# One issue order read from a table, in place of rules: memory-augmented attention plus a SiLU feed-forward layer

## The chip, the cores and the metric

One core of a Trainium2 chip. The time is that of one launch on the device in microseconds (us); lower is better. TensorE does the matmuls, ScalarE (ACT) the activations, VectorE (DVE) and GpSimd (POOL) the element-wise work, SyncE (SP) and ScalarE issue the transfers (DMA).

## The reference, cut to what matters

```python
def reference(A_x, A_wq, A_wk, A_wv, A_wo, A_beta, B_x, B_w1, B_w2):
    xn = _layernorm(A_x)              # 2048 tokens x 512
    return A_x + attention(xn, A_wq, A_wk, A_wv, A_wo, A_beta) + ffn(xn, B_w1, B_w2)

# attention: 32 heads of 16; four segments of 512 tokens. Causal softmax within
# a segment, and a memory M, z carried on from segment to segment:
#   num = phi(q) @ M ; den = phi(q) . z ; o = g*num/den + (1-g)*softmax(...)@v
#   M += phi(k)^T v  ; z += sum phi(k)            phi(t) = t+1 if t>0 else exp(t)
# ffn: silu(xn @ w1) @ w2, 1792 wide
```

The first segment's four token tiles of 128 (x0 to x3) must be loaded, normalised and transposed, and half of w_q loaded, before the first query, key and score matmuls can run.

## The kernel before

The kernel does not emit instructions directly. It builds some 1,700 **tasks** (engine, estimated duration, what they depend on, buffers taken and freed, and a function that emits the instructions). A simulation then picks at each moment a task for each engine, and the functions are called in the simulated order. So the simulation decides only one thing on the chip: the order of the instructions in each engine's stream.

```python
class Sched:
    ENGS = ("SP", "ACTQ", "PE", "ACT", "DVE", "POOL")     # ACTQ: transfers issued by ScalarE
    ...
    def run(self):
        free = {e: 0.0 for e in self.ENGS}                # each has its own time line
        ...
        def pick(e):                                      # rules: scores first, then PV, then by due
            ...
        while left:
            for e in self.ENGS:
                while free[e] <= now + 1e-9:
                    t = pick(e)
                    ...
                    order.append((now, t))

    def load_x(t, n, eng, due, vis, after=()):
        def fn():
            e = nc.sync if eng == "SP" else nc.scalar     # "ACTQ" is ScalarE's own stream
            e.dma_start(...)
    load_x(0, 1, "SP", 0, 3.4)        # last number: when it is taken to have landed
    load_x(1, 1, "ACTQ", 0, 3.55)
    load_x(2, 1, "SP", 0, 3.6)
    load_x(3, 1, "ACTQ", 0, 3.8)
    ...
    ld_q = [load_w(*halves(w_q, A_wq, C2, 0), "ACTQ", 0, 6.4)]
    ...
    # in ln(): the statistics of token tile 2 on ScalarE
    m = A("ACT", 0.6, f_m, [xl[t]], due, label="mean")    # waits for x2
    m = A("ACT", 0.69, f_q, [m], due, label="sq")
    ...
    def first_tile(w, loads, due, label, hf):             # first key or query tile, in halves hf
        b = Buf(banks)
        for j in (2 * hf, 2 * hf + 1):                    # one piece for each token tile
            c, o = slice(j * P, (j + 1) * P), slice((j % 2) * P, (j % 2) * P + P)
            def f(c=c, o=o):
                for ki in range(DT):
                    mm(b.tile[:, o], w[:, ki, 0:P], xnT_b[0].tile[:, ki, c], ki == 0, ki == DT - 1)
            pcs.append(A("PE", 0.3, f, [xnT_done[0][j], loads], ...))
    ...
    for t, k in sc.run():
        k.fn()
```

The softmax here doesn't subtract the row's maximum and nothing guards it: scores larger than these inputs give would overflow.

Of the kernel before, what the change touches and what calls it, by code (L numbers as in the profile page):

```python
# [14 lines left out]
P = 128  # L15
# [25 lines left out]
STARVE = 0.55  # L41
# [4 lines left out]
LOWB = 1  # L46
# [8 lines left out]
LAST = 1  # L55
PVW = 0.0
# [9 lines left out]
SW = 0.1  # L66
SEM = 0.05
SHIFT = {
    "POOL": {
        ("", 4): -31.1, ("kB", 16): 80.6, ("pq", 0): -10.1, ("pq", 2): 18.3, ("pq", 6): 8.4,  # L70
        ("pq", 10): 6.2, ("M52", 1): -7, ("Mbf", 2): 35.4,
    },
    "PE": {
        ("tr", 1): 9.5, ("k1", 0): -13.1, ("k2", 0): 22.9, ("q2", 0): -12.4, ("q3", 0): -0.3,
        ("h0.0", 0): -54.5, ("h0.2", 0): 30.1, ("h0.3", 0): -7.3, ("h0.6", 0): 11.6,
        ("h0.7", 0): 10.6, ("h0.12", 0): -10.2, ("k4", 0): -0.9, ("q6", 0): 9.6, ("k7", 0): -11.8,
        ("v10", 0): -5.8, ("v11", 0): -6.8, ("M0", 0): 5, ("w2.1", 0): 1.8, ("w2.3", 0): -1.8,
        ("wo.3", 0): 20.3, ("h1.1", 0): 7.4, ("h1.3", 0): -16.4, ("h1.4", 0): 3.5,
        ("h1.5", 0): 1.8, ("h1.6", 0): 10.2, ("h1.7", 0): -10.6, ("h1.8", 0): -3.7,
        ("k8", 0): -7.8, ("v22", 0): -12.9, ("M1", 0): -7, ("psN", 0): -5.6, ("w2.4", 0): -30.2,  # L80
        ("w2.7", 0): -3.9, ("wo.4", 0): 28.9, ("wo.5", 0): 3.2, ("wo.6", 0): -27.6,
        ("wo.7", 0): -42.5, ("PV8", 0): 5.8, ("PV9", 0): 8.6, ("PV10", 0): 7.3, ("h2.0", 0): -7.2,
        ("h2.1", 0): 10.7, ("h2.5", 0): -7.9, ("h2.6", 0): -13.3, ("h2.9", 0): 7.9,
        ("q12", 0): -2.8, ("q13", 0): 4.8, ("k14", 0): 1.6, ("k15", 0): 15, ("v32", 0): 26.1,
        ("M2", 0): 29, ("w2.10", 0): 4, ("wo.9", 0): -27.9, ("wo.10", 0): 17.9, ("PV12", 0): 31.2,
        ("PV13", 0): 47.7, ("h3.0", 0): -14.7, ("h3.1", 0): 46.3, ("h3.2", 0): 38.7,
        ("h3.4", 0): -37.3, ("h3.7", 0): 26.5, ("h3.10", 0): -7.1, ("h3.12", 0): 16.4,
        ("h3.13", 0): 40.6, ("outT2", 0): -24.2,
    },
    "DVE": {  # L90
        ("stats", 3): 4.5, ("stats", 10): -3.1, ("xn", 5): -0.9, ("k0", 0): 11.1,
        ("EO", 26): 36.4, ("glu", 45): -20.7, ("tailA", 1): 4.6,
    },
    "SP": {
        ("Z", 15): -16.3, ("Z", 26): 8.7, ("den", 12): -6.9, ("den", 17): 3.5, ("den", 18): -28.9,
        ("den", 20): -20.5, ("out", 10): 21.7, ("mg", 14): 26.1,
    },
}


class Task:
    __slots__ = (
        "eng", "dur", "vis", "fn", "due", "nwait", "ready", "outs", "takes", "frees", "kind",
        "mode", "seq", "started", "end", "tvis", "label", "lock",
# [19 lines left out]
class Ring:  # L124
# [4 lines left out]
    def count(self, t):  # L129
        return sum(1 for a in self.at if a <= t + 1e-9)  # L130

    def take(self, t):
        i = min(range(len(self.at)), key=lambda k: self.at[k])
        assert self.at[i] <= t + 1e-9
        self.at[i] = float("inf")
        return i


class Sched:
    ENGS = ("SP", "ACTQ", "PE", "ACT", "DVE", "POOL")  # L140

    def __init__(self):
        self.tasks = []
        self.log = None
        self.names = {}

    def add(self, eng, dur, fn, deps=(), due=0.0, vis=None, seqdeps=(), takes=(), frees=(),
            kind="", mode=None, keep=0, label="", lock=None):
        t = Task()
        t.eng, t.dur, t.fn, t.due, t.kind, t.mode = eng, dur, fn, due, kind, mode  # L150
# [11 lines left out]
        t.started = False  # L162
        t.seq = len(self.tasks)
        t.label = label
# [9 lines left out]
    def shift(self, table):  # L174
        seen = {}
        for t in self.tasks:
            key = (t.eng, t.label)
            if t.eng == "PE" and t.label not in ("k0", "q0", "tr"):
                n = 0
            else:  # L180
                n = seen.get(key, 0)
                seen[key] = n + 1
            t.due += table.get(t.eng, {}).get((t.label, n), 0.0)

    def run(self):
        free = {e: 0.0 for e in self.ENGS}
        pool = {e: [] for e in self.ENGS}
        for t in self.tasks:
            if t.nwait == 0:
                pool[t.eng].append(t)  # L190
        port = {"DVE": 0.0, "POOL": 0.0}
        left = len(self.tasks)
        now = 0.0
        order = []
        st = {"mode": "full", "exp_next": None, "exps": 0}
        nexps = sum(1 for t in self.tasks if t.kind == "exp")

        def can(t):
            return all(b.idx is not None or b.ring.count(now) > keep for b, keep in t.takes)

        def pick(e):
            c = [t for t in pool[e] if t.ready <= now + 1e-9 and can(t)]
            if not c and e == "PE" and LAST:
                c = [
                    t for t in pool[e] if t.ready <= now + 1e-9 and t.kind == "" and all(
                        b.idx is not None or b.ring.count(now) > 0 for b, _ in t.takes)
                ]
            if not c:
                return None
            if e == "PE":  # L210
                s = [t for t in c if t.kind == "score"]
                if s:
                    return min(s, key=lambda t: t.seq)
                pv = [t for t in c if t.kind == "pv"]
                if not pv and any(
                    t.kind == "pv" and t.ready <= now + 1e-9 and t.due + PVW < now for t in pool[e]
                ):
                    c = [t for t in c if not any(
                        b.idx is None and b.ring is self.names["banks"] for b, _ in t.takes)]
                    if not c:  # L220
                        return None
                if pv:
                    b = min(pv, key=lambda t: (t.due, t.seq))
                    if st["mode"] != "full" or b.due < now:
                        return b
                    c = [t for t in c if t.kind != "pv"]
                    if not c:
                        return b
                return min(c, key=lambda t: (t.due, t.seq))
            if e == "ACT":  # L230
                s = [t for t in c if t.kind == "exp"]
                if s:
                    return min(s, key=lambda t: t.seq)
                b = min(c, key=lambda t: (t.due, t.seq))
                if st["exps"] < nexps and st["exp_next"] is not None:
                    late = 0.06
                    if not any(
                        t.kind != "score" and t.ready <= now + 1e-9 and can(t) for t in pool["PE"]
                    ):
                        late = STARVE  # L240
                    if now + b.dur > st["exp_next"] + late:
                        return None
                return b
            if e == "DVE":
                bk = self.names["banks"]
                if bk.count(now) <= LOWB:
                    f = [t for t in c if any(b.ring is bk for b in t.frees)]
                    if f:
                        return min(f, key=lambda t: (t.due, t.seq))
            return min(c, key=lambda t: (t.due, t.seq))  # L250

        while left:
            for e in self.ENGS:
                while free[e] <= now + 1e-9:
                    t = pick(e)
                    if t is None:
                        if e == "PE" and self.log is not None:
                            self.log.append((now, [
                                (x.label, round(x.ready, 1), [n for n, r in self.names.items() for b, k in x.takes if b.ring is r and b.idx is None and r.count(now) <= k])
                                for x in sorted(pool["PE"], key=lambda x: (x.due, x.seq))[:6]]))  # L260
                        break
                    pool[e].remove(t)
                    d = t.dur
                    if e == "PE":
                        if t.mode != st["mode"]:
                            d += SW
                            st["mode"] = t.mode
                        else:
                            pass
                    if t.lock:  # L270
                        other = "DVE" if e == "POOL" else "POOL"
                        d += max(0.0, port[other] - now)
                        port[e] = now + d
                    t.started = True
                    t.end = now + d
                    t.tvis = now + t.vis + (d - t.dur)
                    free[e] = t.end
                    for b, keep in t.takes:
                        if b.idx is None:
                            b.idx = b.ring.take(now)  # L280
# [1198 lines left out]
```

## Time and profile before

| kernel before | |
|---|---|
| time, median of 3 runs | 226.25 us (226.06 to 226.39) |
| span in the profile | 225.5 us |
| TensorE busy | 213.4 us, 95% |
| first score matmul starts | 11.43 us |
| first score to last matmul | 210.74 us |
| after the last matmul | 3.33 us |

Once the scores have begun, TensorE runs back to back with some 3.6 us of stalls in 210.74. The lines are in the prediction.

ScalarE's stream in the first microseconds: these lines are from its timeline in the profile before. The columns of a timeline are start, duration, engine (ACTq marks a transfer being issued), line, operation, what it writes and reads, and in brackets the idle time ahead of it and what ended that.

```profile
0.79 0.91 ACTq L448 DMA_DIRECT2D x_all<-in_A_x_dram  x2
1.72 0.46 ACTq L459 DMA_DIRECT2D w_q<-in_A_wq_dram  x1
...
4.14 0.63 ACT L636 ACTIVATE scr<-x_all 128x512 bf16<-128x512 bf16 x1 [0.65 <-DMA x_all<-in_A_x_dram]
```

The three transfers (x1 and x3, drawn as one line, then half of w_q) are out by 2.2 us. Only then comes the mean, which waits for x2.

### The profile page before, as it was taken

The page shows a single profiled execution, that of the slowest core. Times are in us where ns is not written, and L with a number is a line of the kernel's source. Part 1 is how long each engine was busy: PE and PEld are TensorE (multiplying, and loading weights), DVE is VectorE, ACT ScalarE, POOL GpSimd, SP SyncE. Part 2 cuts the span into 40 slices and gives each one's busy share as a digit, 9 for nine tenths or more (in the row PEclk, how much of TensorE's full clock was granted, in tenths as well). Part 3 has the DMA queues.
Part 4 walks back from the last instruction along what each step waited for, and adds up shares of the span by engine and source line. Part 5 has one row for each costly group of instructions (what it writes and reads, how often), then busy time and mean ns, then how long its engine had stood idle before and what let it go on. Part 6 is the DMA issues. An engine that isn't in the chain of part 4 may idle for free.

```text
span 225.5 us, 6740 instructions
## 1 busy us (share of the span) xinstructions
PE 213.4 (95%) x2757; PEld 101.1 (45%) x2792; DVE 173.2 (77%) x305; ACT 179.7 (80%) x165; POOL 162.3 (72%) x283
## 2 busy tenths in 40 slices
PE   6899999999999898999999999999999999999994
PEld 6634444435443444444444334344554444444441
DVE  3788988879994789789976849988665784775873
ACT  4498999999988799988989787899898787994000
POOL 4779998889987678999984775968797644568100
PEclk9999999999999999999999999999999999999999
DMA  6974458550265432050364350020523201123202
GB/s 191 366 235 115 99 143 208 65 177 3 47 86 126 93 102 100 22 166 1 49 149 86 71 96 24 0 73 6 178 60 69 97 3 47 55 76 89 74 3 94
DMA packets 30708, 21.11 MB, mean 94 GB/s; under 512 B 15956, under 2 KB 29780, under 8 KB 30676
## 3 DMA queue, kind: packets, MB, share of 16 engines
q1 hardware_dynamic: 29860, 20.14, 34.4%
q10 hardware_dynamic: 816, 0.52, 0.8%
q8 instruction: 22, 0.36, 0.7%
q14 instruction: 10, 0.08, 0.1%
HBM read 11.73 MB, written 2.64 MB: 64 GB/s over the span
## 4 chain that ended last, share of the span: by engine, by line
PE 66%; DVE 8%; ACT 7%; DMA 7%; POOL 5%; issue 4%; SPq 1%; ACTq 0%; POOLq 0%
PE ps L583 54%; PE psS L583 11%; ACT Pt L947 6%; DMA phiK<-pkT 2%; POOL Pt L966 2%; DMA dR<-Zr 2%; DMA R<-dR 1%; POOL kB L824 1%; DMA x_all<-in_A_x_dram 1%; DVE xn L696 1%; DVE pq L760 1%; POOL rstd L685 1%; ACT hT L1239 1%; DVE st L662 1%; DMA Zg<-dZ 1%
## 5 line engine op out<-in xcount | busy, mean ns | idle before, releaser
L947 ACT ACTIVATE Pt<-psS 128x2048 bf16<-128x2048 f32 x72 | 135.4, 1880 | 18.3 <-PE psS L583 15.3
L966 POOL TENSOR_SCALAR_AFFINE_SELECT Pt<-Pt 64x512 bf16<-64x512 bf16 (+1 forms) x144 | 91.2, 634 | 29.3 <-ACT Pt L947 22.1
L583 PE MATMUL ps<-xnT,w 128*128 128x512 bf16 x214 | 57.0, 380 | 0.8 <-issue 0.5
L1243 DVE SCALAR_TENSOR_TENSOR hT<-hT,ps 128x512 bf16<-128x512 bf16 x56 | 36.9, 676 | 15.6 <-ACT hT L1239 15.4
L583 PE MATMUL ps<-w,hT 128*128 128x512 bf16 x185 | 46.6, 380 | 1.5 <-issue 1.4
L1239 ACT ACTIVATE hT<-ps 128x512 bf16<-128x512 f32 x56 | 32.1, 601 | 0.3 <-PE ps L583 0.3
L583 PEld LDWEIGHTS <-hT 128*128 128x128 bf16 x224 | 20.2, 98 | 24.5 <-issue 2.0
L583 PE MATMUL psS<-qT,kB 32*128 32x256 bf16 (+5 forms) x640 | 28.7, 261 | 1.7 <-ACT Pt L947 1.3
L583 PEld LDWEIGHTS <-w 128*128 128x128 bf16 x224 | 19.7, 98 | 23.3 <-issue 2.4
L583 PEld LDWEIGHTS <-kB 32*128 32x128 bf16 x640 | 12.0, 92 | 28.8 <-issue 27.2
L824 POOL TENSOR_SCALAR kB<-kT,pm 128x512 bf16<-128x512 bf16 x30 | 21.8, 736 | 4.1 <-DVE kT L819 2.6
L583 PE MATMUL ps<-Pt,V 64*32 64x256 bf16 (+5 forms) x640 | 19.8, 260 | 0.2 <-DVE N L1224 0.2
L583 PE MATMUL ps<-Pt,VS 64*32 64x256 bf16 (+5 forms) x640 | 18.8, 261 | 0.2 <-DVE acc L1268 0.2
L583 PE MATMUL ps<-xnT,w_q 128*128 128x512 bf16 (+1 forms) x73 | 17.3, 345 | 0.7 <-DVE xnT L724 0.5
L583 PE MATMUL ps<-xnT,w_k 128*128 128x512 bf16 (+1 forms) x73 | 17.3, 344 | 0.5 <-DVE hT L1243 0.4
L583 PEld LDWEIGHTS <-V 64*32 64x32 bf16 x640 | 14.1, 91 | 7.8 <-issue 2.5
L583 PE MATMUL ps<-w_v,xnT 128*128 128x512 bf16 x61 | 15.8, 380 | 0.4 <-issue 0.3
L1145 POOL TENSOR_TENSOR pq<-pq,Dr 128x512 bf16<-128x512 bf16 x12 | 14.1, 1182 | 1.8 <-DMA Dr<-dE 1.2
L583 PE MATMUL ps<-w_o,N 128*128 128x512 bf16 x51 | 14.5, 380 | 0.4 <-issue 0.3
L760 DVE SCALAR_TENSOR_TENSOR pkT<-kT,pkT 128x512 bf16<-128x512 bf16 x12 | 11.6, 963 | 2.2 <-POOL pkT L754 2.2
L1023 DVE CAST N<-ps 128x512 bf16<-128x512 f32 x15 | 10.2, 682 | 3.9 <-PE ps L583 3.8
L583 PEld LDWEIGHTS <-VS 64*32 64x32 bf16 x640 | 12.7, 91 | 0.7 <-DVE acc L1268 0.5
(104 smaller groups left out, 251.4 us busy)
## 6 DMA issues: line engine op xcount, KB each, us to landing
w<-in_B_w_dram SPq DMA_DIRECT2D x4, 896.0 KB
VS<-V SPq DMA_DIRECT2D x8, 264.0 KB
out_dram<-o_t SPq DMA_DIRECT2D x16, 128.0 KB
R<-dR SPq DMA_DIRECT2D x15, 128.0 KB
Dr<-dE SPq DMA_DIRECT2D x12, 128.0 KB
x_all<-in_A_x_dram SPq DMA_DIRECT2D x2, 512.0 KB
N<-O SPq DMA_DIRECT2D x12, 64.0 KB
w_k<-in_A_wk_dram SPq DMA_DIRECT2D x2, 256.0 KB
```

The source lines that it names most:

```text
L583: nc.tensor.matmul(o, lhsT=l, rhs=r, start=start, stop=stop, **k)
L662: nc.vector.bn_stats(out=b.tile[:], in_=xt(t))
L685: nc.gpsimd.tensor_tensor(out=rs, in0=mv[:, t : t + n, 1:2] if first else rs, in1=lnc[:, 0:n, 1:2], op=ALU.pow,)
L696: nc.vector.tensor_scalar(out=xb.tile[:], in0=xt(t), scalar1=mv[:, t, 0:1], scalar2=rstd[:, t, 0:1], op0=ALU.subtract, op1=ALU.mult,)
L760: nc.vector.scalar_tensor_tensor(out=dst_b.tile[:], in0=src_b.tile[:], scalar=0.0, in1=dst_b.tile[:], op0=ALU.max, op1=ALU.add, accum_out=acc,
L824: nc.gpsimd.tensor_scalar(out=kB[u].tile[:, :, KB * r : KB * r + KB], in0=kT[u].tile[:].rearrange("p (a b) -> p a b", b=KB), scalar1=pm[:, ...
L947: nc.scalar.activation(out=pb.tile[:], in_=psS[:], func=AF.Exp, scale=SCALE)
L966: nc.gpsimd.affine_select(out=v, in_=v, compare_op=ALU.is_ge, fill=0.0, base=0, pattern=pat, channel_multiplier=-1,)
L1023: nc.vector.tensor_copy(out=dst.tile[:, dt, :], in_=buf.tile[:])
L1145: nc.gpsimd.tensor_tensor(out=pb.tile[:], in0=pb.tile[:], in1=rb.tile[:], op=ALU.mult)
L1239: nc.scalar.activation(out=hb.tile[:], in_=b.tile[:], func=AF.Tanh, scale=0.5)
L1243: nc.vector.scalar_tensor_tensor(out=hb.tile[:], in0=hb.tile[:], scalar=1.0, in1=b.tile[:], op0=ALU.add, op1=ALU.mult)
```

## The change

The intent: the rules (about 140 lines) and their hand-set corrections go, and with them any doubt about what the order is. A table lists all tasks by number, and the simulation only replays it. Apart from that, tokens 256 to 511 of the first key and query tiles are made in one piece of 256 columns instead of two of 128.

```diff
-STARVE = 0.55 ... LOWB = 1 ... LAST = 1 ... PVW = 0.0
-SHIFT = { "POOL": {...}, "PE": {...}, "DVE": {...}, "SP": {...} }
+ORDER = """
+0 53 1 2 63 14 27 16 15 28 29 30 31 32 33 34 35 36 37 38 39 40 41 42 43 44 45 46 47 48 49 50
+51 52 54 58 59 3 55 56 64 65 66 60 61 4 17 5 6 70 71 57 96 109 67 68 62 110 7 8 69 72 73 74
+... (79 more lines)
+"""
 def run(self):
-    def can(t): ...
-    def pick(e): ...
-    while left: ...
+    for k in ORDER.split():
+        t = self.tasks[int(k)]
+        assert t.nwait == 0
+        now = max(free[t.eng], t.ready)
+        ...
+        order.append((now, t))
@@ first_tile
-    for j in (2 * hf, 2 * hf + 1):
-        c, o = slice(j * P, (j + 1) * P), slice((j % 2) * P, (j % 2) * P + P)
+    for js in ((0,), (1,)) if hf == 0 else ((2, 3),):
+        n = len(js)
+        c, o = slice(js[0] * P, (js[0] + n) * P), slice((js[0] % 2) * P, (js[0] % 2 + n) * P)
```

Tasks 1, 3 and 5 are ScalarE's three transfers: x1, x3 and half of w_q. Tasks 63 and 64 are the mean and the square.

## The prediction

> **What bounds the kernel now.** I read the page first, for the busy shares and the granted clock.
>
> ```profile
> span 225.5 us, 6740 instructions
> PE 213.4 (95%) x2757; PEld 101.1 (45%) x2792; DVE 173.2 (77%) x305; ACT 179.7 (80%) x165; POOL 162.3 (72%) x283
> PEclk9999999999999999999999999999999999999999
> ```
>
> TensorE is busy for 95% of the span at the full clock, 15 points ahead of ScalarE. Next, the busy time in three stretches: up to the first score matmul (11.43 us), from there to the last matmul, and the rest.
>
> ```profile
> 0.00:11.43 11.43, 8.73 (x104) 7.25 (x106) 6.61 (x20) 5.38 (x11) 7.12 (x38) 1.00 0.85 280
> 11.43:222.17 210.74, 204.65 (x2656) 93.82 (x2689) 165.94 (x284) 174.35 (x155) 155.18 (x246) 1.00 0.34 84
> 222.17:225.50 3.33, 0.00 (x1) 0.00 (x0) 0.69 (x1) 0.00 (x0) 0.00 (x0) 1.00 0.24 81
> ```
>
> The second column is the stretch, the third TensorE. In the middle it shows 6.1 us idle of 210.74. The waits of TensorE between 12 and 222 us divide that:
>
> ```profile
> PE ps L583 <- issue: 2.5, 16, 0.2
> PE psS L583 <- ACT Pt L947: 1.3, 3, 0.7
> PE ps L583 <- DVE hT L1243: 0.4, 1, 0.4
> ```
>
> The 16 "issue" gaps are all 0.16 us and stand where one matmul of a group is missing from the trace (groups of "x3" or "x9" where four or ten were issued; 2757 matmuls are recorded, the program has 2793), so they are not idle time. Because a 512-column matmul is drawn 380 ns long but its successor starts 216 ns later, short stalls hide inside the drawn length. So I took the timeline of TensorE and compared starts. The two biggest causes look like this:
>
> ```profile
> 75.18 0.23 PE L583 MATMUL ps<-Pt,V 64*32 64x64 bf16 x4
> 76.11 0.40 PE L583 MATMUL psS<-qT,kB 32*128 32x64 bf16 x8 [0.71 <-ACT Pt L947]
> ...
> 135.32 0.40 PE L583 MATMUL ps<-Pt,V 64*32 64x512 bf16 x4 [0.21 <-DVE N L1224]
> 135.92 0.40 PE L583 MATMUL ps<-Pt,VS 64*32 64x512 bf16 x8 [0.20 <-DVE acc L1268]
> ```
>
> Stalls by differences of starts, beyond 216 ns a matmul and 95 ns for a change from full-array to row-tiled matmuls: 0.8 us at 76.1; 0.43 at 86.5 and 0.34 at 88.9 (scores wait for an exp); 0.55 at 125.5 (a bank held by a gate product, behind a reciprocal that waited for a DMA); 0.27 and 0.57 at 135 (the two banks of a PV); 0.27 at 139; some 0.4 in three small ones near 107, 167 and 180. Together 3.6 us. The rest of the 210.7 us is matmuls back to back: 207.1 us that no order takes away.
>
> **What the Trainium skill says.** "Perfetto Trace Analysis", section Identifying the Most-Contended Engine, calls matmul busy time a bad measure because matmuls are pipelined. This trace agrees (380 ns drawn, 216 ns apart), and so I count stalls by starts. "TensorE: Matmul & The Clock Gate", Part 3, section The mechanism, says that matmuls start and end strictly in program order. The trace agrees in that a PV waiting for a bank at 135.3 stops all that stands behind it; so the table's order is what TensorE will do, right or wrong. "Perfetto Trace Analysis", section Per-engine timelines (DVE / Act Engine Instruction), says a ScalarE instruction is pushed into a wait queue and the sequencer then decodes the next. No run here shows it yet; it matters for the loads below.
>
> **The change part by part.** Work removed: almost none. The second halves of the first key and query tiles become 4 matmuls of 256 columns each in place of 8 of 128: 8 matmuls and 8 weight loads fewer. At about 55 ns from start to start for 128 columns (four in 0.22 us at 10.24) and twice that for 256, it is the same array time, 0.44 us a tile. It does cost readiness: the piece of the third token tile could run at 9.12 before, beside the last transpose; now all waits for the fourth.
>
> The start. In the built order, VectorE evicts the last transpose before the first query half and key copies, where before it stood behind both; that eviction ran at 9.77, with its matmuls done about 9.2. Moving it up gives about 0.5 us on the pieces that waited for it at 10.24. The merged pieces give back 0.2 (query) on the path to the first score. The score was at 11.43 because the query's second half was evicted at 10.66 to 11.03. I put it at 11.1, with four value matmuls done ahead of it in place of three key matmuls: 0.2 us more. Gain: 0.3 + 0.2 = 0.5 us.
>
> Against that, one thing the diff does not show. On ScalarE's queue, before had the loads of x tile 1, x tile 3 and half of w_q first and then the table load and the mean; the new order puts the x3 load behind the table load and the mean (which waits for x2), and the w_q load behind the square. If the sequencer runs past waiting instructions, little is lost. If it blocks, x3 is issued near 4.7 in place of 1.23 and w_q near 5.6 in place of 1.72; w_q landed near 7.0 and would land near 8.5, and the first query piece, at 7.42 before, holds up the third and fourth transposes behind it. By those numbers the first score comes at 11.5 to 12.3. Half and half: the expected gain of the start is 0.5 in one case, about -0.4 in the other, so roughly 0.
>
> The middle. I counted in the two built orders. Changes of array mode between groups: 164 in both; leaving full mode, which is what costs 95 ns, 73 times against 74. Nothing there. What the order can win is the 3.6 us of stalls. The score, exp, score loop has a least period of 2.38 us (0.45 from score to exp, 1.93 from exp to the next score, both the smallest of 71), and exp occupies 1.77 us with 0.48 for each further ScalarE operation. Before had two cycles in a row with only 1.84 and 1.70 us of TensorE work between scores (the PV of tile 5 put next to a lone matmul): the stalls at 86.5 and 88.9. In the new order no cycle has under 2.34 us. That removes 0.77, and the small ScalarE-bound ones probably, 0.3. The other 2.5 us come from the norm chain, phi's transposed store and banks; several were put elsewhere (the gate product no longer behind the reciprocal at that place, the second PV of a pair no longer back to back with its scores). I give half, 1.25 us. Sum so far 2.3 us.
>
> What it adds: accumulation groups (four or fourteen matmuls into one bank) that are broken by other groups rise from 22 to 68 of 129, and there are 40 places with three open groups where there was none. There are four banks, and a PV needs two. A bank that is held longer has less room for a late eviction. I allow 0.4 us of new stalls.
>
> The tail. From the last PV on, the same 56 output matmuls, the same 8-deep last run on the last tile (10 before), then one eviction (0.69) and one store: 3.33 us as now. The reciprocals (3.37 us) and four following VectorE operations (1.44) plus three products start after 26 cover matmuls (5.6 us); that just fits. 0.
>
> Sum: 226.25 - 0.0 - 2.3 + 0.4 = 224.3; since an order as long as this was presumably looked for with more care than I give it, I take 224.1 us.
>
> **Rivals.** (1) Bank pressure: the interleaved groups meet evictions later than planned. For it: the 40 places with three open groups, DVE at 77%, and that before's worst stalls at 125 and 135 were such. Against: VectorE is idle for 23% of the span, and in before only 1.5 us of stalls were late evictions. It would add 1 to 3 us: 225 to 227. (2) The late loads on ScalarE's queue move the first score by 1 to 2 us, and as TensorE is dense afterwards, this goes into the end one for one: 225 to 226.3. For: the order itself. Against: the skill's account of the wait queue. (3) All stalls go: 226.25 - 3.6 - 0.5 = 222.1. For: an order fixed by hand or search can look ahead, which a rule can't. Against: DMA landings vary, and a fixed order follows estimates. (4) ScalarE becomes the bound: five cycles in a row (13 to 17) have two further operations. Each needs 1.77 + 0.96 = 2.73 us against periods of 2.63 to 2.81, so the delay stays under the 0.2 us of room. Nothing.
>
> **Range and chances.** The floor is (3), 222.1. The ceiling is (1) with (2), near 227. Eight in ten: 222.6 to 226.2. Faster by 2% means under 221.7, below the floor: 0.04. Slower by 2% means over 230.8, 4.5 us of new stalls with no gain: 0.02. Within 2%: 0.94.
>
> **What would show it.** The time to the first score matmul (11.43 before): 11.1 says the sequencer ran past the waits; 11.5 or later, with x3 and w_q issued after the mean, says it blocked. The stretch from the first score to the last matmul (210.74): near 209 if the stalls fell to 1.7 us; the waits of TensorE should name ScalarE's exp for under 0.5 us in place of 1.3. Wrong would be: TensorE idle before PV or before first matmuls of groups, released by VectorE evictions, of over 2 us (rival 1), or no idle at all and under 208 us (rival 3).

## The result and the profile after

| | before | after |
|---|---|---|
| time, median (6 runs each) | 226.32 us (225.71 to 227.82) | 233.59 us (232.49 to 234.10) |
| ratio | | 1.0307, interval 1.0267 to 1.0347 |
| span in the profile | 225.5 us | 231.9 us |
| mean granted clock | 1.000 | 0.985 |

Ratios here are the mean time of one kernel's runs over that of the other's runs of the same rounds, so they are not quite the ratio of the medians quoted. Executions over 1.5% slower than the fastest of the same kernel are left out of the means. The change made the kernel 3% **slower**; the prediction had 224.1 us and gave that 2%.

From the page of the profile after:

```profile
span 231.9 us, 6699 instructions
PE 217.0 (94%) x2751; PEld 103.1 (44%) x2784; DVE 172.7 (74%) x305; ACT 180.7 (78%) x165; POOL 163.1 (70%) x283
PEclk9959999999999999999999999999999999999999
```

The third slice of the clock, about 11.6 to 17.4 us, shows 5: TensorE ran at half speed there. The same three stretches as before (start, end and length, then the busy time of PE, PEld, DVE, ACT and POOL, the clock, the DMA share and GB/s):

```profile
0.00:18.23 18.23, 11.42 (x96) 9.98 (x98) 6.24 (x19) 5.66 (x11) 6.04 (x34) 0.81 0.76 245
18.23:228.50 210.27, 205.62 (x2657) 93.12 (x2688) 165.79 (x286) 175.01 (x155) 157.03 (x249) 1.00 0.30 77
228.50:231.90 3.40, 0.00 (x0) 0.00 (x0) 0.67 (x1) 0.00 (x0) 0.00 (x0) 1.00 0.31 107
```

Set against the stretches before (11.43, 210.74 and 3.33) that is +6.80, -0.47 and +0.07, together the 6.4 us between the two spans. (The medians differ by 7.3: the execution profiled before was one of 227.24 us, 0.9 above its median.) **The whole loss between the two profiles lies ahead of the first score matmul.** ScalarE's timeline at the start, after:

```profile
3.91 0.63 ACT L559 ACTIVATE scr<-x_all 128x512 bf16<-128x512 bf16 x1 [1.39 <-DMA x_all<-in_A_x_dram]
3.92 0.33 ACTq L371 DMA_DIRECT2D x_all<-in_A_x_dram  x1
...
4.67 0.72 ACT L566 ACTIVATE scr<-x_all,nbias 128x512 bf16<-128x512 bf16 x1
4.67 0.39 ACTq L382 DMA_DIRECT2D w_q<-in_A_wq_dram  x1
```

The load of x3 is issued at 3.92, in the moment in which the mean ahead of it starts, and that of w_q when the square starts. They had been out at 1.23 and 1.72. What that does downstream, from the timelines of VectorE and TensorE after:

```profile
10.75 0.69 DVE L585 BATCH_NORM_STATS2 st<-x_all 128x6 f32<-128x512 bf16 x1 [3.95 <-DMA x_all<-in_A_x_dram]
...
13.25 0.61 PE L506 MATMUL ps<-xnT,w_q 128*128 128x128 bf16 x4 [4.72 <-DMA w_q<-in_A_wq_dram]
...
18.23 0.39 PE L506 MATMUL psS<-qT,kB 32*128 32x512 bf16 x4
```

and the same three events before:

```profile
6.49 0.68 DVE L662 BATCH_NORM_STATS2 st<-x_all 128x6 f32<-128x512 bf16 x1
...
7.42 0.40 PE L583 MATMUL ps<-xnT,w_q 128*128 128x128 bf16 x4
...
11.43 0.40 PE L583 MATMUL psS<-qT,kB 32*128 32x512 bf16 x4
```

So a delay of 2.7 to 3.0 us at the issue has become 4.3 at the statistics of x3, 5.8 at the first query piece and 6.8 at the first score. Two things swell it. First, each transfer takes longer: w_q took 8.6 us from its issue to its first matmul, where before it took 5.7. Second, TensorE idles until 13.25, and then the clock is down. Of five stretches of two microseconds, after, four:

```profile
8.00:10.00 2.00, 0.38 (x4) 0.21 (x3) 0.00 (x0) 0.58 (x2) 0.00 (x0) 1.00 1.08 359
10.00:12.00 2.00, 0.00 (x0) 0.00 (x0) 1.18 (x4) 0.00 (x0) 0.07 (x1) 0.66 1.12 337
...
14.00:16.00 2.00, 1.99 (x16) 1.66 (x16) 0.76 (x2) 0.92 (x2) 0.67 (x4) 0.50 1.04 261
16.00:18.00 2.00, 1.79 (x10) 1.20 (x9) 0.82 (x2) 0.61 (x3) 0.00 (x0) 0.63 0.02 5
```

The third number from the right is the clock: 0.66 in the idle stretch, 0.50 when the work returns. The one next to it is the share of the DMA engines: it is about 1 up to 16 us, so they are full until then, with the later loads that SyncE has queued as well.

### The profile page after: what moved, and what is told of

Same layout as the page of the kernel before. It is cut to its first block, busy times and chain, and to the rows that moved or that the text cites. A ratio compares the mean times of both kernels' runs of the same rounds, so it can differ in the third digit from the quotient of the medians.

```text
span 231.9 us, 6699 instructions
## 1 busy us (share of the span) xinstructions
PE 217.0 (94%) x2751; PEld 103.1 (44%) x2784; DVE 172.7 (74%) x305; ACT 180.7 (78%) x165; POOL 163.1 (70%) x283
## 4 chain that ended last, share of the span: by engine, by line
PE 71%; POOL 9%; DMA 8%; DVE 5%; ACT 3%; issue 2%; SPq 0%; POOLq 0%; DVEq 0%
PE ps L506 60%; PE psS L506 11%; DMA w_q<-in_A_wq_dram 4%; POOL Pt L891 3%; POOL kB L749 3%; ACT Pt L872 2%; DMA xnT<-xn 2%; DMA Zg<-dZ 2%; POOL rstd L608 1%; POOL pq L677 1%; DMA x_all<-in_A_x_dram 1%; DVE pq L683 1%; DVE xn L619 1%; DVE hT L1167 1%; DVE Zf L1106 0%
## 5 line engine op out<-in xcount | busy, mean ns | idle before, releaser
L891 POOL TENSOR_SCALAR_AFFINE_SELECT Pt<-Pt 64x512 bf16<-64x512 bf16 (+1 forms) x144 | 90.1, 633 | 29.2 <-ACT Pt L872 24.1
L506 PE MATMUL ps<-xnT,w 128*128 128x512 bf16 x210 | 58.7, 380 | 1.4 <-DVE hT L1167 0.6
L506 PE MATMUL ps<-w,hT 128*128 128x512 bf16 x187 | 50.5, 380 | 0.6 <-issue 0.3
L506 PEld LDWEIGHTS <-w 128*128 128x128 bf16 x224 | 20.4, 98 | 24.5 <-issue 3.7
L506 PE MATMUL ps<-xnT,w_q 128*128 128x512 bf16 (+2 forms) x68 | 18.4, 374 | 5.7 <-DMA w_q<-in_A_wq_dram 4.7
L506 PEld LDWEIGHTS <-kB 32*128 32x128 bf16 x640 | 11.6, 92 | 26.1 <-issue 24.4
L506 PE MATMUL ps<-xnT,w_k 128*128 128x512 bf16 (+2 forms) x71 | 18.8, 364 | 1.0 <-ACT xnT L645 0.5
L506 PE MATMUL ps<-w_v,xnT 128*128 128x512 bf16 x61 | 17.7, 384 | 0.1
L585 DVE BATCH_NORM_STATS2 st<-x_all 128x6 f32<-128x512 bf16 x15 | 10.2, 682 | 7.5 <-DMA x_all<-in_A_x_dram 7.5
L506 PE MATMUL ps<-w_o,N 128*128 128x512 bf16 x54 | 15.0, 380 | 0.2 <-issue 0.2
L744 DVE CAST kT<-ps 128x512 bf16<-128x512 f32 x15 | 10.2, 682 | 3.5 <-PE ps L506 2.9
```

The lines of the kernel that those rows point to most:

```text
L506: nc.tensor.matmul(o, lhsT=l, rhs=r, start=start, stop=stop, **k)
L585: nc.vector.bn_stats(out=b.tile[:], in_=xt(t))
L744: ev = [A("DVE", 0.6, lambda: nc.vector.tensor_copy(out=kT[u].tile[:], in_=b.tile[:]), [g], due + 1.5, takes=(kT[u],), frees=(b, kT[u]), l ...
L891: nc.gpsimd.affine_select(out=v, in_=v, compare_op=ALU.is_ge, fill=0.0, base=0, pattern=pat, channel_multiplier=-1,)
```

## The experiments

**The theory**: ScalarE's stream is one stream. The two loads behind waiting activations go out late, and that is the whole loss. **Rivals**: (a) the loads cost part, and the rest comes from the new order of the matmuls at the start; (b) only one of the two loads matters, the other is hidden behind it; (c) the merged pieces cost; (d) the long landing is fixed, or else comes from the backlog on the DMA engines; (e) the lowered clock is a real part of the loss, or only stands beside a wait that is there anyway. The first four runs shared one chip (before there: 226.98 us median, 226.19 to 228.01). All others ran on a second, less steady chip (before there: 225.89 to 228.29).

### 1. Both loads back to the front

```diff
-0 53 1 2 63 14 27 16 15 ...
-51 52 54 58 59 3 55 56 64 65 66 60 61 4 17 5 6 ...
+0 53 1 2 3 5 63 14 27 16 15 ...
+51 52 54 58 59 55 56 64 65 66 60 61 4 17 6 ...
```

> The changed kernel with only two entries of its table moved: the loads of x tile 3 and of half of w_q are issued on ScalarE's queue right after the load of x tile 1, as in the kernel before; all else as changed. Theory L (the late loads are the whole loss): the first score starts at 10.9 to 11.5 us in place of 18.23, no clock dip, and the time is 225 to 226.5 us. Rival M (the new middle or the merged pieces lose too): first score early, but the stretch from first score to last matmul grows above 211.5 us, time over 227.5. Rival K (the loads were only half of it, other things of the new start are late too): first score still at 13 or later.

Measured: 226.61 us (226.28 to 226.81), 0.9973 of before (0.9947 to 0.9999), clock 1.0. The query pieces and the first score on TensorE's timeline of this run:

```profile
8.46 0.39 PE L504 MATMUL ps<-xnT,w_q 128*128 128x128 bf16 x4
...
11.57 0.40 PE L504 MATMUL psS<-qT,kB 32*128 32x512 bf16 x4
```

Two numbers of some 1,700 moved, and the first score is at 11.57 instead of 18.23. All of the loss is gone. That leaves nothing for rivals (a) and (c).

### 2 and 3. One load at a time

In the second run only task 5 (w_q) moves to the front, in the third only task 3 (x3).

> The changed kernel with only the w_q load moved ahead of the mean; the x tile 3 load still stands behind the mean. If one late load alone is enough (x3 landed between 9 and 10.7 us and its tile needs about 2.9 us from there to its transpose): first score at 14 to 16.5 us, time 228 to 231. If w_q alone was the cause: first score under 12, time under 226.5.

Measured: 233.36 us (232.96 to 234.06), ratio 1.0273 (1.0241 to 1.0306). The x3 load went out at 4.82 (the mean started at 4.81), its statistics ran at 11.08, and the first score at 17.86.

> The changed kernel with only the x tile 3 load moved ahead of the mean; the w_q load still stands behind the square. w_q is then alone in ScalarE's ring and should land earlier than 12.7 us, at 9 to 12. First score at 14 to 16 us, time 229 to 232. If x3 alone was the cause: first score under 12, time under 226.5.

Measured: 234.66 us (232.79 to 235.18), ratio 1.0313 (1.0270 to 1.0355). The w_q load went out at 4.87 (square at 4.86), the first query piece ran at 12.73, and the first score at 17.60.

Each late load **alone** costs nearly the whole, more than expected (14 to 16.5 us). The two paths (x3 through statistics, normalising and transposes; w_q straight to the query) end nearly together, so the costs do not add up and no half repair helps. Rival (b), that only one of the two matters, is false for either: each is enough by itself.

### 4. The same two delays put into the kernel before

```diff
-    for t, k in sc.run():
+    todo = [k for _, k in sc.run()]
+    for load, ahead in (("x3", "mean"), ("w", "sq")):
+        k = next(k for k in todo if k.eng == "ACTQ" and k.label == load)
+        todo.remove(k)
+        todo.insert(1 + next(i for i, x in enumerate(todo) if x.label == ahead), k)
+    for k in todo:
         k.fn()
```

> The kernel before with only these two loads put behind the mean and the square on ScalarE's queue; every other engine's order is as before. Theory L: x3 is issued when the mean starts (about 4 us) and w_q when the square starts (about 4.7), they land near 10 and 12.7, the first score moves from 11.43 to about 18, and the time is 232 to 234 us. Rival M: under 229 us, as the loss would lie in the new order itself.

Measured: 233.42 us (232.34 to 234.89), ratio 1.0277 (1.0235 to 1.0319), first score at 17.54. From ScalarE's timeline:

```profile
3.91 0.63 ACT L636 ACTIVATE scr<-x_all 128x512 bf16<-128x512 bf16 x1 [1.39 <-DMA x_all<-in_A_x_dram]
3.92 0.34 ACTq L448 DMA_DIRECT2D x_all<-in_A_x_dram  x1
```

The old order with the two loads late is as slow as the new one. With run 1 this shows the cause from both sides. The loads have nothing else to wait for: in the program that the kernel after builds, neither of the two transfers has a semaphore to wait for, and each stands directly behind its activation.

### 5. Without the backlog of later loads

The kernel after, with SyncE's later loads (w_1 and what follows) held back: a copy of 32 bytes that reads the square's output stands ahead of them.

```diff
-    ld_1 = [load_w(*halves(w_1, B_w1, F2, 0), "SP", 0.1, 9.5)]
+    spare = sb([1, 16], BF16, "spare")
+    def f_w1():
+        nc.sync.dma_start(out=spare[:], in_=scr[0:1, 0:16])
+        dst, src = halves(w_1, B_w1, F2, 0)
+        nc.sync.dma_start(out=dst, in_=src)
+    ld_1 = [A("SP", 0.5, f_w1, due=0.1, vis=9.5, label="w")]
```

> The changed kernel, its two loads still late on ScalarE's queue, but SyncE's queue holds back everything after w_v (3.3 MB of w_1, x and second halves) until the square has ended, by a 32-byte copy that reads the square's output. If the late loads land so late because 1.8 MB and more of SyncE's loads are already in the DMA engines' rings ahead of them: x3 lands near 6.5 us in place of 10.7 and w_q near 7.5 in place of 13.2, first score near 12.5, time 226 to 228. If the lateness of a load issued at 4 us is its own (slow small rows): x3 and w_q land as before, time 232 or more.

Measured: 229.46 us (227.35 to 231.26, four runs, one of them slow), ratio of the fast ones 1.0050 (0.9977 to 1.0122), clock 1.0, first score at 12.98. TensorE's timeline of the run:

```profile
8.92 0.40 PE L512 MATMUL ps<-xnT,w_q 128*128 128x128 bf16 x4 [1.31 <-DMA w_q<-in_A_wq_dram]
```

Here w_q went out at 4.87, later than in the kernel after, and its first matmul ran 4.05 us later instead of 8.58. The last packet on ScalarE's transfer queue came at 8.5 instead of 12.7. So the long landing is backlog: the loads that SyncE had issued meanwhile were ahead on the same DMA engines. "DMA: Bandwidth & Descriptors", section Issuing engines are not separate DMA queues, says so of the Trainium skill's pages: transfers run on the same 16 engines whichever engine starts them. This run agrees. Lateness of under 3 us costs nearly 7 mostly because the place in the line of transfers is lost as well: without the backlog the first score is 5.25 us earlier (12.98 against 18.23), the clock's share included, which the next two runs take apart. That settles (d).

### 6 and 7. Filling TensorE's wait

The kernel after, with extra matmuls (identity times identity, results unused) ahead of the first query piece: 42 of them, then 90.

```diff
+    fill = 42 if label == "q0" and js == (0,) else 0      # second run: 90
-    def f(c=c, o=o):
+    def f(c=c, o=o, fill=fill):
+        for _ in range(fill):
+            mm(psS[:, 3, 0:P], ident[:], ident[:], True, True)
         for ki in range(DT):
```

> The changed kernel with 84 idle-identity matmuls of 128 columns ahead of the first query piece... in fact 42 of them, about 4.6 us at 0.11 us each, in the wait for w_q (8.5 to 13.2 us). If the granted clock of 0.5 from 11 to 17 us came from that idle stretch, the clock stays 1.0, and the work from 13.2 us to the first score takes about 3.2 us in place of 5.0: first score near 16.5, time 231.5 to 232.3. If the clock dip costs nothing on the path: time as the changed kernel's, 233.3.

Measured: 235.99 us (234.55 to 236.43), ratio 1.0378 (1.0326 to 1.0430). The fillers took 56 ns each and not 110, so they were over in 2.5 us. TensorE still waited 3.33 us for w_q, and the clock fell again (0.60 from 14 to 17 us); first score 17.92. For the clock's share this was **inconclusive**, by my error in the size (the expectation's "84" is another slip in the same sum).

> The kernel after with 90 extra 128-column matmuls (results unused) ahead of the first query piece, where the run with 42 had them over in 2.5 us. At the 56 ns measured there they last 5.0 us, from about 7.9 to 12.9, close to the first query piece at 13.25. If the fallen clock between 10 and 18 us is a real share of the loss (estimate: 2 to 2.5 us, as some 20 matmuls ran 100 ns longer each and others less): granted clock 1.0 throughout, first score at 15.8 to 16.8 in place of 18.23, time 231 to 232.3. If the score waits for the token chain of tile 3 and not for TensorE's speed: first score stays at 17.5 or later, time 233 to 235.

Measured: 232.25 us (230.69 to 234.26, the longest in the slow state), ratio 1.0180 (1.0112 to 1.0249), which by the 2% rule is unclear against the kernel before; clock 1.00 in every stretch up to 20 us. TensorE's timeline:

```profile
7.30 5.19 PE L506 MATMUL psS<-ident 128*128 128x128 bf16 x90
12.59 0.40 PE L506 MATMUL ps<-xnT,w_q 128*128 128x128 bf16 x4
...
15.71 0.39 PE L506 MATMUL psS<-qT,kB 32*128 32x512 bf16 x4
```

From the first query piece to the first score it took 4.98 us in the kernel after (13.25 to 18.23), 4.24 with 42 fillers, and 3.12 with 90. In run 1, where nothing waited, it had taken 3.11 (8.46 to 11.57). So the clock cost 1.87 us, and useless work bought it back. (w_q landed 0.66 us earlier in this execution than in the profile after; that is not the fillers' doing.) Between run 1 and the kernel after, the 6.66 us at the first score divide into 4.79 of waiting for the first query piece and 1.87 of half clock. That settles (e): a real part, somewhat over a quarter. It is read at the first score, in one profiled execution of each kernel; the whole times do not show it as cleanly, as a stall further on (see runs 9 to 12) made both filled runs longer.

### 8. The old order in the table, with the merged pieces only

The order of before, written into the table word for word, so that only the merge of the second halves remains.

> The order of the kernel before, written into the table word for word (all five engines' instructions compared, the same), with the second halves of the first key and query tile merged: the other part of the change alone. Theory: a wait for the fourth transpose for work that ran 1 us earlier, first score 0.2 us later, time +0.0 to +0.4 us. If the merge saved something: -0.2 us or more.

Measured: 226.69 us (225.40 to 229.04, the longest slow), ratio 0.9969 (0.9925 to 1.0012). Nothing measurable either way: the interval is -1.7 to +0.3 us. (The only profile is of the slow execution, where w_q landed later, at 8.2 against 7.0 before, and the first score came at 12.74; it does not time the merge.) Reading the order from a table does nothing by itself either; it only matters what stands in it.

### 9 to 12. Is there a better table?

With its loads in front, the table kernel had 209.49 us from the first score to the last matmul, 1.25 less than before. That is one execution of each; run 4, with the old order, had 210.56, and runs 2 and 3, with the new, 210.39 and 209.97, so 1.25 is the most that the order can be said to have won. Four further moves aimed at its four longest stalls there (0.48, 0.37, 0.68 and 0.55 us): the second half of w_k ahead of that of w_1 among the loads; one transfer behind its neighbour; a gate constant and a product hT earlier on VectorE; two denominator tasks later.

```diff
-... 9 10 21 114 115 111 112 113 11 101 ...        +... 9 11 10 21 114 115 111 112 113 101 ...
-448 ahead of 623;        25 and 736 behind 476;           1575 1576 ahead of 1374
+448 right behind 449;    25 ahead of 516, 736 of 476;     1575 1576 behind 1380
```

> The changed order with the loads first and four more entries moved: w_k's second half ahead of w_1's (0.48 us stall at 17.5), the second swapped-value copy ahead of the two merges (0.37 at 77), a gate product and the gate columns ahead of a reciprocal that waits for a DMA (0.68 at 78.5), and the last denominator matmuls seven matmuls later (0.55 at 187.5). If each of these stalls is on the path, 2.1 us go: 224.3 to 225.0, about 1.0% under the kernel before. If stalls behind them take their place: 225.8 or more.

Measured: 226.25 us (225.17 to 227.34), ratio 0.9965 (0.9922 to 1.0008), stretch 208.64. The four stalls were gone, 2.1 us, but only 0.85 remained as gain. New ones had come up, the longest 0.63 us at 81.9. On the same chip, five rounds each, run 1's kernel again, this one again, and one with a fifth move (tasks 723 and 724, the hT behind that new stall, ahead of 418):

> The kernel after with the two loads moved to the front of ScalarE's order, once more with five rounds, beside its two successors on the same chip. Theory late loads: 225.8 to 227 and 0.995 to 1.000 of the kernel before, as in its first run (0.9973). First score 11.5 to 11.6, first score to last matmul 209.5.

Measured: 228.16 us (226.08 to 228.91), ratio 1.0024 (0.9975 to 1.0073).

> The same with the four moves, second time. If the 0.85 us that its profile showed in the middle is real, it is 0.996 of the kernel a1_again in the same rounds, near 225.4 to 226; if its stalls only come out elsewhere in most executions, no difference from a1_again.

Measured: 226.87 us (225.52 to 227.32), ratio 0.9974 (0.9932 to 1.0016). This overlaps a1_again, so the gain of the four moves is not shown.

> The four moves and a fifth: the tanh and the gating product hT of one column block go ahead of the phi(k) product on VectorE, which there waited for GpSimd. The stall of 0.63 us at 81.9, which the four moves had brought in, should go: first score to last matmul 208.0 to 208.3 in place of 208.64, time 0.4 to 0.6 us under m1_again. If a stall merely moves on again (phi(k) a gap later, or the next PV): no change.

Measured: 227.17 us (226.88 to 227.71), ratio 1.0005 (0.9965 to 1.0046). The stall at 81.9 fell from 0.63 to 0.15 us, but the stretch was 210.08, longer than the 208.64 of m1_four_moves. No version clearly beats the kernel before.

Why a stall removed doesn't show can be read from two executions of one kernel, the one with four moves. The first, span 223.6, VectorE:

```profile
86.77 0.48 DVE L1131 TENSOR_TENSOR N<-N,R 128x512 bf16<-128x512 bf16 x1
...
91.35 0.42 DVE L1131 TENSOR_TENSOR N<-N,R 128x512 bf16<-128x512 bf16 x1
```

The second, span 225.5, VectorE, TensorE and then GpSimd:

```profile
86.88 0.82 DVE L1131 TENSOR_TENSOR N<-N,R 128x512 bf16<-128x512 bf16 x1 [0.37 <-DMA R<-dR]
...
92.21 1.47 DVE L1131 TENSOR_TENSOR N<-N,R 128x512 bf16<-128x512 bf16 x1
```

```profile
91.14 0.38 PE L504 MATMUL ps<-xnT,w_q 128*128 128x512 bf16 x1 [0.53 <-DVE O L945]
...
94.33 0.59 PE L504 MATMUL ps<-w_o,N 128*128 128x512 bf16 x2 [0.65 <-DVE qT L790]
```

```profile
91.93 1.47 POOL L889 TENSOR_SCALAR_AFFINE_SELECT Pt<-Pt 64x512 bf16<-64x512 bf16 x2 [1.73 <-ACT Pt L870]
```

In the second one a transfer (R, the reciprocals spread over the rows) came 0.37 us too late. VectorE stood still, because the order is fixed, and all its later work shifted. The product that had run ahead of GpSimd's mask now met it (two masks, from 91.93 to 93.40) and took 1.47 us instead of 0.42, until 93.68. The query's eviction stood behind it, and TensorE lost 0.53 and 0.65, together 1.2 of the 1.8 us by which its stretch is longer here (210.47 against 208.64). "SBUF — State Buffer", section Who interferes with whom, has the reason for the 1.47: a VectorE instruction with two inputs in SBUF contends with a GpSimd instruction that reads SBUF, and the second to come is blocked until the first is done. The numbers here agree. The same pair of stalls is in five of the eleven profiles of the new order and its variants: in all five where R was waited for by 0.3 us or more (runs 5, 6, 7, 11 and 12, all on the second chip), and in none of the six where it was 0.2 or not at all. At 1.2 us it is also most of what run 7's stretch (211.7, in spite of its full clock) and run 6's (211.6) have over the 210.27 of the kernel after. Whether it is why run 1's kernel took 226.1 to 226.5 in two executions and 228 to 229 in the other four of its second trial is likely but not shown: only the first of the six was profiled, a quick one without the stalls.

## Why the prediction was wrong, point by point

- **"w_q landed near 7.0 and would land near 8.5"**, the cost of the late loads, is the step that failed. Even for the case that the sequencer blocks, the prediction put the first score at 11.5 to 12.3; it came at 18.23, some 6 us later. I also had this as rival (2), "by 1 to 2 us". The issue times were close (x3 put at 4.7 and found at 3.92; w_q at 5.6 and 4.67). The landing was at 12.7. I added a small delay to the old landing as if the line of transfers would wait. In run 5, without the backlog, w_q did land at 8.5; the backlog is worth 4.5 us from issue to use. And I left out the clock, 1.87 us. So rival (2) should have read 6.8 us.
- **"Half and half ... so roughly 0"** averaged two answers to a yes-or-no question: does ScalarE's sequencer run past a waiting instruction to a transfer behind it? It does not. The transfer went out when the activation ahead of it started: 3.92 after 3.91, 4.67 with 4.67, 4.82 after 4.81, 4.87 after 4.86. The averaging alone did little harm: by the prediction's own sizes the right answer would have added only about 0.4 us.
- **The order itself "gives about 0.5 us" at the start**: not so. With the loads in front the first score came at 11.57 and 11.42, against 11.43 before, where I had 11.1.
- **The middle, "-2.3" and "+0.4"**: the direction was right, the size too large. Run 1's stretch is 1.25 shorter than before, and that of the kernel after 0.47, where I had 1.9 in sum. The exp waits went as worked out: 1.3 us before, no such line in the list after. From the waits of TensorE between 12 and 230 us, after:

```profile
PE ps L506 <- DVE hT L1167: 0.6, 1, 0.6
PE ps L506 <- DVE pq L683: 0.5, 1, 0.5
PE ps L506 <- DMA xnT<-xn: 0.5, 1, 0.5
```

  These, the longest of the list besides the wait for w_q (and lines of "issue"), took their place. The second and the third are inputs that VectorE or a transfer makes too late. The first is rival (1), banks held too long, at a small size:

```profile
86.43 1.02 PE L506 MATMUL ps<-xnT,w 128*128 128x512 bf16 x3 [0.62 <-DVE hT L1167]
```

  This matmul does not read hT. It waits for its bank, which the gate product (hT from hT and ps) still reads; that product stands behind a reciprocal that waited for a DMA, the pattern that the prediction saw at 125.5 before and noted as gone from there. A like wait of 0.3 us is at 32.02. Together that is about 0.9 us, under the 2 us that would have made rival (1) the cause. The "half" of 2.5 us that I let the order win was a guess without a working.
- **The tail, 0**: right (3.40 against 3.33 us). **The merged pieces, 0.2**: too small for run 8 to show or to refute.
- **The range** had a ceiling, "(1) with (2), near 227", that took rival (2) at 2 us at most and did not even add the two: rival (1) alone was put at up to 227, so that both make about 229. (Two slips besides, without effect: the program before has 2792 matmuls and not 2793; and not only leaving full-array mode costs some 95 ns but the return as well, 93 to 105 ns by the starts in the trace before. Both orders have as many changes.) The sign that I named ("11.5 or later, with x3 and w_q issued after the mean, says it blocked") was the right one to look for.

## What to carry to other kernels

When an order is reshuffled, look first at what each engine's instruction stream now has **in front of its transfers**: a transfer behind a waiting activation waits too, and it loses its place among the transfers as well. A model that gives one engine's transfers a time line of their own can't see this. A prediction that hangs on a yes-or-no question should size the costly answer with the most care: here it was seen, and put at about 1 us instead of 6.8. And a table that fixes the order is worth only as much as its slack: here a transfer 0.37 us late cost TensorE 1.2 us, about as much as the 1.25 us that the order had won at most.

## What the Trainium skill lacked or had wrong

- "Perfetto Trace Analysis", Per-engine timelines (DVE / Act Engine Instruction), has the sequencer decode the next instruction once one is in the wait queue. It does not say what a transfer on ScalarE does behind a waiting activation. Here it was issued only when the activation started, within 0.01 us, in seven kernels (the kernel after and runs 2 to 7; for instance 3.92 after 3.91 and 4.67 with 4.67), with 3.95 and 4.72 us of waiting downstream. One can read the page as promising the opposite, as I half did.
- "DMA: Bandwidth & Descriptors" has the shared engines, but none of its sections that I read gives the price of a late issue under backlog: 8.58 us from the issue of w_q's half to its first matmul with later loads ahead, 4.05 without them, for the same 256 KB.
- "TensorE: Matmul & The Clock Gate", Part 1, What's actually happening, puts the fall to half clock after at least one idle window of about 3.4 us. In the kernel after, TensorE's last matmul ended at 8.53 and the clock was at half from about 10.64 (an estimate from the mean of 0.60 in the stretch 10.6 to 10.8), 2.1 us later. It came back at about 17.47, 4.2 us after work returned at 13.25. So a shorter wait than the page's window was enough here; in runs 3 and 6 the clock fell 1.7 and 2.6 us after the last matmul (9.89 after 8.17, 12.96 after 10.35).
